# Softmax attention without row maxima, its exponentials shared by two engines, and linear attention laid under it by a list scheduler

## The chip, the cores and the metric

The program runs on one core of one Trainium2 chip. A core has five instruction streams that run side by side and meet only in semaphores: TensorE (PE, matrix products into PSUM), VectorE (DVE), ScalarE (ACT), GpSimd (POOL) and SyncE (SP, which here issues the DMAs). Each stream is executed in the order in which it was written. The metric is the device time of one execution in microseconds (us).

## The reference

Two attention layers over 2048 positions, 512 features and 32 heads of 16 features; their outputs stand side by side.

```
A:  q, k, v = split(x @ wqkv);  scores = q k^T * 0.25
    o = softmax(scores) v;      a = o @ wo
B:  q, k, v = split(x @ wqkv);  pq = q @ w_phi;  pk = k @ w_phi        (16x16 for each head)
    phi(t) = [softmax(t), softmax(-t)]                                 (32 features)
    kv = sum over positions of phi(pk) v;  z = sum over positions of phi(pk)
    o = phi(pq) kv / (phi(pq) z + 1e-6);   b = o @ wo
out = concat(a, b)                                                     (2048 x 1024, bfloat16)
```

A's softmax takes 32 x 2048 x 2048 exponentials, which are 1,048,576 columns on 128 partitions. All else is small beside it.

## The kernel before

**Units.** A is cut into 32 units: 8 groups of four heads times 4 blocks of 512 queries. A unit has 16 key tiles of 128 keys. The four heads of a group lie at partitions 0, 32, 64 and 96 of `QT` and `KT`, 16 rows of features each, so that four scores matmuls can use four row strips of PE's array.

**Two passes over the scores.** The first pass exists only for the row maximum. `emit_m1` (the matmul is L611) writes scores with queries on the partitions, two heads at a time into a pair of PSUM banks, and `emit_r1` (L623) has DVE reduce these 128x1024 scores to their maxima. `emit_mchain` (L634 on DVE, L644 to L646 on POOL) makes two bfloat16 numbers of the maximum, and `emit_qb` and `emit_qe` (L654, L661, L672) add them to `QT` as two extra features, so that the second pass yields scores with the maximum taken off. The second pass has keys on the partitions: `emit_m2` (L692), one 128x512 block for each head, `emit_exp` (L703) on ACT, and `emit_pv` (L718), four products in four column strips of the array, which add up in PSUM bank 7 over the 16 key tiles. `VP` holds ones beside the values, so that the sums of the softmax come out with the numerators.

```
t = P.op("act", lambda e: e.activation(                                        # emit_exp, L703
    pT[:, slot, :], PS[:, bank, :], ACT.Exp, scale=0.25), [m2_t[B], slot_reader.get(slot)])
...
r1[q1] = P.op("dve", lambda e: e.tensor_reduce(                                # emit_r1, L623
    part[:, u % 2, qt, 2 * half:2 * half + 2, kc], PS[:, 2 * half:2 * half + 2, :],
    AX.X, ALU.max), deps)
```

**End of a unit.** `emit_xev` (L755) copies the sums and numerators to `X`, four DMAs (L759) spread the sums to the partitions of the numerators in `Yd`, ACT makes reciprocals of them as Exp(-Ln) (L769, L777), and POOL multiplies (L779).

**Order.** A hand-written loop over slots sets it: a slot holds one pair of L611 matmuls and their reduction, two blocks of the second pass (43 slots behind), a `PV` group every second slot, and what is left over of PE's time is filled by `emit_fill` (L734, L745) with products of zeros. Projections (L231, L249) stand ahead and in the first slots.

**B.** Its inputs are loaded when A's projections are through. Its key side and 12 of 16 tiles of its query side are hooks in the slots behind A's last row maximum (`T0`), the others follow after A. For each tile of 128 positions `fm0` to `fm3` take maximum, minimum, two subtractions (L374 to L379), an exponential (L388), sums (L397), reciprocals (L400) and a product on POOL (L409).

Of the kernel before, what the change touches and what calls it, by code (L numbers as in the profile page):

```python
# [1 line left out]

# [3 lines left out]
ACT = mybir.ActivationFunctionType  # L6
ALU = mybir.AluOpType
AX = mybir.AxisListType
BF = mybir.dt.bfloat16
F32 = mybir.dt.float32  # L10


class _Tok:
# [35 lines left out]
class _Plan:  # L49
# [19 lines left out]
    def dma(self, queue_key, dma_key, fn, deps=()):  # L69
        q = self.streams[queue_key]  # L70
        d = self.streams[dma_key]
        need = q.merge(deps)
        d.seq += 1
        clock = dict(q.known)
        clock[dma_key] = d.seq
        q.items.append((fn, need, dma_key))
        return _Tok(dma_key, d.seq, clock)

    def emit(self, key, eng):
        for fn, need, inc_key in self.streams[key].items:  # L80
# [10 lines left out]
        return s.seq * s.step  # L91


def bass_concat_heads__softmax_full_mha__linear_kernel_hedgehog__prompt_kernel(
    nc, A_x, A_wqkv, A_wo, B_x, B_wqkv, B_w_phi, B_wo, out
):
    S = 2048
    H = 32
    assert tuple(A_x.shape) == (1, S, 512) and tuple(B_x.shape) == (1, S, 512)
# [18 lines left out]
    with contextlib.ExitStack() as es:  # L118
        block = es.enter_context(nc.Block())

        def sb(name, shape, dt):
            return es.enter_context(nc.sbuf_tensor(name, shape, dt))

        P = _Plan()
        for key in ("pe", "act", "dve", "pool"):
            P.add_stream(key, es.enter_context(nc.semaphore("s_" + key)))
        P.add_stream("sp", None)

        def dsem(name):
            P.add_stream(name, es.enter_context(nc.semaphore("d_" + name)), 16)  # L130
            return name

        PS = es.enter_context(nc.psum_tensor("PS", [128, 8, 512], F32))
        bank_reader = {}

        ones_t = sb("ones_t", [128, 128], BF)
# [718 lines left out]
        NR = 4  # L855
# [118 lines left out]

        final_waits = [k for k, s in P.streams.items() if s.step == 16 and s.seq > 0]

        @block.sync
        def _(e):
            P.emit("sp", e)
            for k in final_waits:  # L980
                e.wait_ge(P.streams[k].sem, P.total(k))

        @block.tensor
        def _(e):
            P.emit("pe", e)

        @block.scalar
        def _(e):
            e.preload_act_table_set("natural_log_exp_and_others")
            P.emit("act", e)  # L990

        @block.vector
        def _(e):
            P.emit("dve", e)

        @block.gpsimd
        def _(e):
            P.emit("pool", e)


# [26 lines left out]
```

## Time and profile before

| | |
|---|---|
| median of 3 runs | 1420.08 us (1416.58 to 1423.36) |
| profiled execution, span from the first to the last instruction | 1415.5 us |
| busy: PE, DVE, ACT, POOL | 1240.7, 1324.3, 1269.5, 156.8 us |
| row maxima, L623 on DVE | 1024 instructions, 1165.5 us busy |
| exponentials, L703 on ACT | 2048 instructions, 1087.7 us busy |
| products of zeros, L734 and L745 on PE | 5644 instructions, 473.7 us busy |

The profile gives one execution; its own time is its span, 1415.5 us, and 4.6 us less than the median of the runs. "Busy" is the union of an engine's instructions, so it is less than count times mean duration where instructions overlap at their edges. Line numbers (L623) are those of the kernel before; those of the changed kernel are named as such.

### The profile page before, as it was taken

The page shows a single profiled execution, that of the slowest core. Times are in us where ns is not written, and L with a number is a line of the kernel's source. Part 1 is how long each engine was busy: PE and PEld are TensorE (multiplying, and loading weights), DVE is VectorE, ACT ScalarE, POOL GpSimd, SP SyncE. Part 2 cuts the span into 40 slices and gives each one's busy share as a digit, 9 for nine tenths or more (in the row PEclk, how much of TensorE's full clock was granted, in tenths as well). Part 3 has the DMA queues.
Part 4 walks back from the last instruction along what each step waited for, and adds up shares of the span by engine and source line. Part 5 has one row for each costly group of instructions (what it writes and reads, how often), then busy time and mean ns, then how long its engine had stood idle before and what let it go on. Part 6 is the DMA issues. An engine that isn't in the chain of part 4 may idle for free.

```text
span 1415.5 us, 32468 instructions
## 1 busy us (share of the span) xinstructions
PE 1240.7 (88%) x13964; PEld 372.4 (26%) x13996; DVE 1324.3 (94%) x1333; ACT 1269.5 (90%) x2474; POOL 156.8 (11%) x257
## 2 busy tenths in 40 slices
PE   5998999998999988888888899998888998988766
PEld 2332322222222222222222222222222222233244
DVE  1499999999999999999999999999999999688978
ACT  3648999999999999999999999999999999877557
POOL 5000000000000000000000000000000000034432
PEclk9999999999999999999999999999999999999989
DMA  5006000000000000000000000000000000000001
GB/s 119 1 1 106 20 5 6 5 5 5 5 5 5 5 5 5 5 5 5 5 5 5 6 5 5 5 6 5 5 3 5 5 5 6 5 20 16 20 26 50
DMA packets 34480, 18.88 MB, mean 13 GB/s; under 512 B 25120, under 2 KB 32288, under 8 KB 34336
## 3 DMA queue, kind: packets, MB, share of 16 engines
q1 hardware_dynamic: 34336, 16.81, 5.3%
q8 instruction: 109, 1.79, 0.5%
q14 instruction: 35, 0.29, 0.1%
HBM read 3.16 MB, written 4.19 MB: 5 GB/s over the span
## 4 chain that ended last, share of the span: by engine, by line
DVE 81%; PE 11%; ACT 5%; issue 1%; SPq 1%; POOL 1%; DMA 0%; DVEq 0%; ACTq 0%; POOLq 0%
DVE part L623 76%; PE PS L249 4%; ACT pT L703 3%; PE PS L366 1%; PE PS L231 1%; PE PS L611 1%; PE PS L505 1%; DVE statK L397 1%; DVE tbK L379 1%; DVE statK L374 1%; DVE statK L375 1%; PE PS L420 1%; PE PS L692 1%; PE PS L960 1%; ACT ebK L388 0%
## 5 line engine op out<-in xcount | busy, mean ns | idle before, releaser
L623 DVE TENSOR_REDUCE part<-PS 128x2 f32<-128x1024 f32 x1024 | 1165.5, 1219 | 42.1 <-PE PS L611 38.5
L703 ACT ACTIVATE pT<-PS 128x512 bf16<-128x512 f32 x2048 | 1087.7, 605 | 30.2 <-PE PS L692 7.8
L692 PE MATMUL PS<-QT,KT 32*128 32x512 bf16 x2048 | 508.0, 386 | 20.3 <-ACT pT L703 12.5
L611 PE MATMUL PS<-KT,QT 32*128 32x512 bf16 x2048 | 397.3, 385 | 79.5 <-DVE part L623 67.9
L734 PE MATMUL PS<-zmv,ones_t 128*32 128x512 bf16 x5228 | 439.2, 383 | 0.0
L611 PEld LDWEIGHTS PS<-KT,QT 32*128 32x128 bf16 x2048 | 96.3, 91 | 532.9 <-DVE part L623 505.9
L718 PE MATMUL PS<-pT,VP 128*32 128x512 bf16 x2048 | 205.4, 391 | 17.0 <-ACT X L755 17.0
L692 PEld LDWEIGHTS PS<-QT,KT 32*128 32x128 bf16 x2048 | 140.4, 91 | 101.0 <-ACT pT L703 81.7
L779 POOL TENSOR_TENSOR QT<-X,Yd 128x256 bf16<-128x256 f32 x64 | 46.3, 723 | 740.7 <-ACT Yd L777 740.7
L734 PEld LDWEIGHTS PS<-zmv,ones_t 128*32 128x32 bf16 x5228 | 99.5, 95 | 97.0 <-issue 97.0
L718 PEld LDWEIGHTS PS<-pT,VP 128*32 128x32 bf16 x2048 | 52.6, 92 | 135.7 <-issue 109.8
L644 POOL TENSOR_SCALAR stage<-mrow 128x16 bf16<-128x16 f32 x32 | 10.0, 311 | 398.9 <-DVE mrow L634 398.9
L388 ACT ACTIVATE ebK<-tbK 128x1024 bf16<-128x1024 f32 x28 | 29.8, 1063 | 25.0 <-DVE tbK L379 24.6
L409 POOL TENSOR_TENSOR phikK<-ebK,statK 128x512 bf16<-128x512 bf16 x36 | 37.2, 1055 | 69.8 <-DVE statK L400 65.8
L249 PE MATMUL PS<-xAT,WKp 128*128 128x512 bf16 x125 | 30.7, 395 | 16.0 <-DVE WKp L200 15.9
L261 ACT ACTIVATE KT<-PS,bias_k 128x512 bf16<-128x512 f32 x32 | 22.0, 687 | 22.7 <-PE PS L249 22.7
L374 DVE TENSOR_REDUCE statK<-PS 128x32 f32<-128x512 f32 x28 | 18.6, 665 | 23.9 <-PE PS L366 23.7
L745 PE MATMUL PS<-zmv,ones_t 128*32 128x512 bf16 x416 | 34.5, 383 | 2.5
L257 ACT ACTIVATE QT<-PS 128x512 bf16<-128x512 f32 x32 | 19.1, 597 | 19.3 <-PE PS L249 19.3
L366 PE MATMUL PS<-WKp,xAT 128*128 128x512 bf16 x119 | 33.4, 402 | 2.6 <-issue 1.3
L249 PE MATMUL PS<-xAT,WQp 128*128 128x512 bf16 x125 | 33.7, 390 | 0.4 <-issue 0.3
L397 DVE TENSOR_REDUCE statK<-ebK 128x64 f32<-128x1024 bf16 x28 | 33.5, 1196 | 0.0
(89 smaller groups left out, 620.8 us busy)
## 6 DMA issues: line engine op xcount, KB each, us to landing
Yd<-X SPq DMA_DIRECT2D x128, 32.0 KB, 2.0
out_dram<-OA SPq DMA_DIRECT2D x16, 128.0 KB, 1.7
out_dram<-pT SPq DMA_DIRECT2D x16, 128.0 KB, 1.7
wA<-in_A_wqkv_dram SPq DMA_DIRECT2D x3, 512.0 KB, 4.3
WOp<-in_A_wo_dram SPq DMA_DIRECT2D x4, 128.0 KB, 6.2
wA<-in_B_wqkv_dram SPq DMA_DIRECT2D x1, 512.0 KB, 5.0
BD<-in_B_w_phi_dram SPq DMA_DIRECT2D x32, 0.5 KB, 1.5
woB<-in_B_wo_dram SPq DMA_DIRECT2D x1, 512.0 KB, 3.3
```

The lines of the kernel that those rows point to most:

```text
L249: tok = P.op("pe", lambda e, ct=ct: e.matmul(PS[:, b, :], wpad[:, ct, g, :], xAT[:, ct, c * 512:(c + 1) * 512], start=(ct == 0), stop=(ct ...
L366: tok = bank_task(bank, 4, lambda e, b, ct: e.matmul(PS[:, b, :], xBT[:, ct, st * 128:(st + 1) * 128], Wf[:, x, ct, :], start=(ct == 0), s ...
L397: t6 = P.op("dve", lambda e: e.tensor_reduce(ss, ebuf[:, ie, :].rearrange("p (g f) -> p g f", f=16), AX.X, ALU.add), [ctx["exp"]] + users. ...
L409: t8 = P.op("pool", lambda e, a=a: e.tensor_tensor(dv[:, a], ev4[:, a], rs3[:, a].unsqueeze(2).broadcast_to([128, 32, 16]), ALU.mult), [ct ...
L611: tok = P.op("pe", lambda e, r=r: e.matmul(PS[:, r, :], QT[32 * r:32 * r + 32, g, q0:q0 + 128], KT[32 * r:32 * r + 32, g, kc * 512:(kc + 1 ...
L623: r1[q1] = P.op("dve", lambda e: e.tensor_reduce(part[:, u % 2, qt, 2 * half:2 * half + 2, kc], PS[:, 2 * half:2 * half + 2, :], AX.X, ALU ...
L692: m2_t[B] = P.op("pe", lambda e: e.matmul(PS[:, bank, :], KT[32 * r:32 * r + 32, g, kt * 128:(kt + 1) * 128], QT[32 * r:32 * r + 32, g, c ...
L703: exp_t[B] = P.op("act", lambda e: e.activation(pT[:, slot, :], PS[:, bank, :], ACT.Exp, scale=0.25), [m2_t[B], slot_reader.get(slot)])
L718: tok = P.op("pe", lambda e, B=B, r=r: e.matmul(PVB[32 * r:32 * r + 32, :], VP[:, kt, 4 * g + r, :], pT[:, B % RING, :], start=(kt == 0), ...
L734: P.op("pe", lambda e, cq=cq: e.matmul(PVB[32 * cq:32 * cq + 32, :], ones_t[:, 0:32], zmv[:, :], start=False, stop=False, tile_position=(0 ...
L745: P.op("pe", lambda e, cq=cq: e.matmul(PS[32 * cq:32 * cq + 32, bank, :], ones_t[:, 0:32], zmv[:, :], start=True, stop=True, tile_position ...
L779: t = P.op("pool", lambda e: e.tensor_tensor(QT[:, g, lo:lo + 256], X[:, ub, sl], Yd[:, ub, sl], ALU.mult), [ex, xev_t[u], last_m2[u]])
```

## The change

The kernel of before stays in the program as `_general`, with every name prefixed, behind a branch. Ahead of it stands a new function, `_main_path`, which computes the whole result in another way; every engine then loads a flag and enters `_general` only if the flag is set.

- A without maxima: the first pass, the chain behind it, the two extra features and the products of zeros are gone. A scores block is made once, with keys on the partitions.
- On ACT an exponential now covers a pair of banks, 128x1024.
- Four of 16 key tiles of a unit (`DK`) are meant for DVE. `tensor_scalar` computes `ya * score + yb` from PSUM and writes it as uint16 (L613 of the changed kernel); those bits, read as bfloat16, are 2 to a power, with a straight line between powers of two. To even out the line's error six such values with shifted phases are added up: five more `tensor_scalar` add a whole number to the uint16 tile of 128x2048 and clamp it (L625), each shifted tile goes into a `PV` group of its own with values scaled to fit (`VJ`). A key tile on DVE so takes 2 conversions, 5 additions and 6 `PV` groups. Where ACT is through first, it takes a tile from DVE's list; in the built order that happens for one tile.
- A unit ends in a copy by DVE (L550), four DMAs that broadcast one row of sums to 16 partitions (L558) and four that collect the sums (L564), a `reciprocal` of 128x512 on DVE (L570) and a product on POOL (L572).
- B loses its maxima and minima, too. Its key side takes exponentials from PSUM on ACT (L781), sums and reciprocals on DVE (L787, L790), the product on POOL (L792); its query side takes transposed features (L874, L884), reciprocals and products from PSUM on DVE (L900, L903), nine small operations for each tile on POOL (L918 to L933).
- The order comes from a list scheduler, `_Sched`: each piece of work is a task with an engine, a duration from a table of constants in the code, its predecessors and the buffers that it needs; at each step the task that can start first is placed, by priority of its stream where several can. B's tasks have lower priorities than A's. The emitted streams are fixed; the chip waits by semaphores alone.
- At the end DVE counts sums that lie between 2^-40 and 2^40 (L983 to L993) and sets the flag.

```diff
+    def qk_task(u, kt, half, need, nbank):
+        g, c = units[u]
...
+            return e.matmul(PS[:, b, :], KT[32 * r:32 * r + 32, g, kt * 128:(kt + 1) * 128],
+                            QT[32 * r:32 * r + 32, c, g // 2, :], start=True, stop=True, tile_position=(32 * r, 0))
+        return _Task("pe", 0.28, pe_group(2, mm), [q_ready[(g // 2, c)], k_ready[(g, kt // 4)]], lat=0.2, need=need)
...
+    def act_kt(u, kt):
+        exps = []
+        for half in range(2):
+            qk = qk_task(u, kt, half, [("A", A_bank, 1, 1)], lambda t: 2 * t.res["A"].idx)
...
+                return e.activation(pT[:, t.res["p"].idx, :], PS[:, b:b + 2, :].rearrange("p a n -> p (a n)"),
+                                    ACT.Exp, scale=0.25)
+            exps.append(put(ac_ex, _Task("act", 0.957, one("act", ex_emit), [qk], lat=0.12,
+                                         need=[("p", pt_sl, 1, 1)], rel=[lambda qk=qk: [qk.res["A"]]])))
...
+    def dve_kt(u, kt):
+        npv[u] += _NPH - 1
+        firsts = []
+        for half in range(2):
+            qk = qk_task(u, kt, half, [("D", D_bank, 2, 1)], lambda t: 4)
...
+                return e.tensor_scalar(rg[:, firsts[0].res["i"].idx, 1024 * half:1024 * half + 1024],
+                                       PS[:, 4:6, :].rearrange("p a n -> p (a n)"), ya, yb, ALU.mult, ALU.add)
+            firsts.append(put(dv_a, _Task("dve", 1.19, one("dve", cv), [qk], lat=0.1,
+                                          need=[("i", ri_sl, 1, _NPH)] if half == 0 else [],
...
+        for j in range(1, _NPH):
+            ad = put(dv_ad, _Task("dve", 0.61, one("dve", lambda e, t, j=j: e.tensor_scalar(
+                rg[:, t.res["j"].idx, :], rg[:, firsts[0].res["i"].idx, :], float(sh[j]), 32767.0, ALU.add, ALU.min)), firsts, lat=0.1,
+                need=[("j", rj_sl, 1, 1)], rel=[lambda: [firsts[0].res["i"]]]))
+            put(pe_pd, pv_task(u, kt, [ad, vj_ready[(kt, j)]],
+                               lambda h, j=j: VJ[:, j - 1, k, 17 * h:17 * h + 32],
...
+            rc = put(dv_n, _Task("dve", 0.62, one("dve", lambda e, t: e.reciprocal(
+                Yd[:, yi(), :], Yd[:, yi(), :])), [sh_], lat=0.1))
+            mul[u] = put(po_n, _Task("pool", 1.4, one("pool", lambda e, t: e.tensor_tensor(
+                OT[:, g, :], X[:, xi, :], Yd[:, yi(), :], ALU.mult)), [rc] + op_done.get(c - 1, []), lat=0.1,
...
+        def guard(e, fn):
+            with e.If(e.value_load(flag[0:1, 0:1])):
+                for k in ends:
+                    e.wait_ge(P0.streams[k].sem, P0.total(k))
+                fn(e)
```

In the built order the changed path has 254 conversions, 635 additions, 32 long reciprocals and 140 copies of 512 columns from PSUM on DVE; 770 exponentials of 1024 columns on ACT; 1024 pairs of scores matmuls and 1147 groups of `PV` on PE.

What the order does on DVE: before, the end of A's row maxima and the first tile of B (`part` maxima by block, `mrow` maxima by unit, `statK` and `tbK` B's maxima and differences):

```order
L623 TENSOR_REDUCE part<-PS 128x2 [waits s_pe] x30
L634 TENSOR_REDUCE mrow<-part 128x16 [waits s_dve]
L374 TENSOR_REDUCE statK<-PS 128x32 [waits s_pe]
L375 TENSOR_REDUCE statK<-PS 128x32
L377 TENSOR_TENSOR tbK<-PS,statK 128x512 [waits s_dve]
L379 TENSOR_TENSOR tbK<-statK,PS 128x512 [waits s_dve]
```

Now, around the end of a unit in the middle of A (`X` and `Yd` as before, `rg` the uint16 tiles):

```order
L550 COPY X<-PS 128x512 [waits s_pool,d_col1,s_pe]
L613 TENSOR_SCALAR rg<-PS 128x1024
L625 TENSOR_SCALAR rg<-rg 128x2048
L613 TENSOR_SCALAR rg<-PS 128x1024 [waits s_pe]
L570 RECIPROCAL Yd<-Yd 128x512 [waits d_sh0]
L625 TENSOR_SCALAR rg<-rg 128x2048 [waits s_pe]
L625 TENSOR_SCALAR rg<-rg 128x2048
```

The reductions are gone, B's tiles no longer stand behind them, and the reciprocal stands in line with conversions and additions, three instructions behind the copy whose row it needs by DMA (`d_sh0`).

What it does on PE: before, a stretch of the middle of A (`zmv` and `ones_t` are the products of zeros):

```order
L611 MATMUL PS<-KT,QT 128x512 [waits s_dve]
L611 MATMUL PS<-KT,QT 128x512
L692 MATMUL PS<-QT,KT 128x512 [waits s_act] x2
L718 MATMUL PS<-pT,VP 32x512 x4
L734 MATMUL PS<-zmv,ones_t 32x512 x4
```

Now, a stretch of the middle of A (L515 scores, L523 `PV`, from ACT's `pT` or DVE's `rg`):

```order
L515 MATMUL PS<-QT,KT 128x512 [waits s_act]
L515 MATMUL PS<-QT,KT 128x512
L523 MATMUL PS<-pT,VP 32x512 x4
L523 MATMUL PS<-rg,VP 32x512 x4
L523 MATMUL PS<-rg,VJ 32x512 [waits s_dve]
L523 MATMUL PS<-rg,VJ 32x512 x3
L515 MATMUL PS<-QT,KT 128x512 [waits s_act]
L515 MATMUL PS<-QT,KT 128x512
L515 MATMUL PS<-QT,KT 128x512 [waits s_dve]
L515 MATMUL PS<-QT,KT 128x512
```

Scores for ACT and scores for DVE, and the products of both, now stand in one line, so that a matmul that waits for DVE holds up the scores for ACT that stand behind it.

More of the change, by code (lines that the diff above doesn't have):

```diff
@@ L10 @@
 F32 = mybir.dt.float32
+U16 = mybir.dt.uint16
+I32 = mybir.dt.int32
 class _Tok:
@@ L91, in total, with __init__, take, drop @@
         return s.seq * s.step
-def bass_concat_heads__softmax_full_mha__linear_kernel_hedgehog__prompt_kernel(
-    nc, A_x, A_wqkv, A_wo, B_x, B_wqkv, B_w_phi, B_wo, out
-):
+class _Slot:
+    __slots__ = ("idx", "free", "toks", "left", "next")
+    def __init__(self, idx):
+        self.idx = idx
+        self.free = 0.0
+        self.toks = []
+        self.left = 0
+        self.next = []
+    def take(self, n):
+        toks = self.toks
+        self.toks = []
+        self.next = []
+        self.left = n
+        return toks
+    def drop(self, tok, end):
+        self.next.append((tok, end))
+        self.left -= 1
+        if self.left == 0:
+            self.free = max(e for _, e in self.next)
+            self.toks = [k for k, _ in self.next]
@@ new lines, with __init__ @@
+class _Task:
+    __slots__ = ("eng", "dur", "lat", "deps", "emit", "need", "tok", "end", "res", "then", "rel", "done", "pre")
+    def __init__(self, eng, dur, emit, deps=(), lat=0.0, need=(), rel=(), then=None, pre=()):
+        self.eng = eng
+        self.dur = dur
+        self.lat = lat
+        self.emit = emit
+        self.deps = [d for d in deps if d is not None]
+        self.need = list(need)
+        self.rel = list(rel)
+        self.then = then
+        self.pre = list(pre)
+        self.res = {}
+        self.tok = None
+        self.end = None
+        self.done = False
```

775 lines of the change are left out of this document (763 added, 12 removed).

## The prediction

> **What bounds the kernel now.** I read the page first (busy shares and the chain that ended last), then the chain in order of time, then the groups of instructions by form, then single stretches.
>
> ```profile
> span 1415.5 us, 32468 instructions
> PE 1240.7 (88%) x13964; PEld 372.4 (26%) x13996; DVE 1324.3 (94%) x1333; ACT 1269.5 (90%) x2474; POOL 156.8 (11%) x257
> DVE  1499999999999999999999999999999999688978
> ACT  3648999999999999999999999999999999877557
> DVE 81%; PE 11%; ACT 5%; issue 1%; SPq 1%; POOL 1%; DMA 0%; DVEq 0%; ACTq 0%; POOLq 0%
> ```
>
> Three engines look full, but the chain runs over DVE for 81% of the span. The stretch that repeats shows why:
>
> ```profile
> 609.39 36.20 DVE part L623 x32
> 300.00:336.30 36.30, 32.65 (x397) 8.80 (x396) 36.30 (x34) 35.38 (x72) 2.29 (x5) 1.00 0.02 5
> ```
>
> The first line is the chain in order of time, the second a window of one unit (PE, PEld, DVE, ACT, POOL busy, granted clock, DMA share, GB/s). A unit takes 36.3 us, all of them DVE's: 32 row-max reductions at 36.20/32 = 1.131 us. ACT has 35.38 of 36.30 and would bind next. Outside this stretch lie loads and projections, the first two digits of DVE's row, and the bulk of B, its last six, where neither engine stays at 9.
>
> **Prices.** Groups by form, columns: count, then busy us and mean ns of one.
>
> ```profile
> L623 DVE TENSOR_REDUCE part<-PS 128x2 f32<-128x1024 f32 x1024 | 1165.5, 1219 | 42.1 <-PE PS L611 38.5 <-PE PS L692 0.9
> L397 DVE TENSOR_REDUCE VP<-KT 128x64 f32<-128x1024 bf16 x4 | 4.8, 1210 | 0.0
> L939 DVE TENSOR_TENSOR VP<-PS,VP 128x256 bf16<-128x256 f32 x32 | 12.1, 420 | 0.6
> L400 DVE RECIPROCAL statK<-statK 128x64 f32<-128x64 f32 x28 | 15.5, 553 | 1.0
> L935 DVE RECIPROCAL VP<-VP 128x32 f32<-128x32 f32 x16 | 5.6, 353 | 0.5
> L200 DVE COPY WQp<-wA 128x2048 bf16<-128x2048 bf16 x1 | 0.7, 694 | 3.7 <-DMA wA<-in_A_wqkv_dram 3.7
> L200 DVE COPY WKp<-wA 128x2048 bf16<-128x2048 bf16 x1 | 0.9, 883 | 5.3 <-DMA wA<-in_A_wqkv_dram 5.3
> L703 ACT ACTIVATE pT<-PS 128x512 bf16<-128x512 f32 x2048 | 1087.7, 605 | 30.2 <-PE PS L692 7.8
> L672 ACT ACTIVATE QT<-PS 128x256 bf16<-128x256 f32 x64 | 25.1, 392 | 0.0
> L354 ACT ACTIVATE VP<-PS 128x1024 bf16<-128x1024 bf16 x16 | 16.4, 1032 | 1.5 <-PE PS L909 1.5
> L779 POOL TENSOR_TENSOR QT<-X,Yd 128x256 bf16<-128x256 f32 x64 | 46.3, 723 | 740.7 <-ACT Yd L777 740.7
> L409 POOL TENSOR_TENSOR QT<-KT,VP 128x512 bf16<-128x512 bf16 x8 | 8.3, 1057 | 32.2 <-DVE VP L933 32.2
> L644 POOL TENSOR_SCALAR stage<-mrow 128x16 bf16<-128x16 f32 x32 | 10.0, 311 | 398.9 <-DVE mrow L634 398.9
> ```
>
> And single instructions of DVE, PE and SP in order of time (start, us):
>
> ```profile
> 1394.86 0.68 DVE L375 TENSOR_REDUCE VP<-PS 128x32 f32<-128x512 f32 x1
> 1395.46 0.68 DVE L377 TENSOR_TENSOR KT<-PS,VP 128x512 f32<-128x512 f32 x1
> 599.72 0.39 PE L692 MATMUL PS<-QT,KT 32*128 32x512 bf16 x1
> 600.03 0.62 PE L734 MATMUL PS<-zmv,ones_t 128*32 128x512 bf16 x8
> 601.01 0.40 PE L718 MATMUL PS<-pT,VP 128*32 128x512 bf16 x4
> 601.23 0.39 PE L734 MATMUL PS<-zmv,ones_t 128*32 128x512 bf16 x4
> 623.97 2.41 SPq L759 DMA_DIRECT2D Yd<-X  x4
> ```
>
> Queued DVE instructions follow each other about 0.08 us sooner than they last (1.131 against 1.219; starts 0.60 apart against 0.68), ACT's by 0.605 - 1087.7/2048 = 0.074. I count steps start to start.
>
> **Removed.** Row maxima, 1024 x 1.131 = 1158 us of DVE, and with them the binding chain; half of PE's scores; on ACT the Ln and Exp of each unit, and B's passes of maxima and differences.
>
> **ACT now.** 256 columns more cost 605 - 392 = 213 ns, so 1024 columns last 605 + 426 = 1031 ns (L354's 1032 agrees) and step at 0.957. 770 of them are 737 us in place of 1088; four evacuations of 1024 columns and 96 other instructions of 512 at 0.53 are 55 more. ACT: 792 us.
>
> **DVE now.**
> (a) Conversions: 254, one float column from PSUM per step as the reduction reads it, at 1.13: 287 us.
> (b) Additions: 635 over 2048 two-byte columns in SBUF. Nothing in this trace adds uint16. From below the copy of 2048 bfloat16 columns, 694 ns, step 0.61, 390 us; from above one column at a time as L397 reads bfloat16, twice 1.21 less the fixed part, 2.26 us, 1435 us. I take the copy: one source, one constant pair, SBUF to SBUF, the same 2048 columns of two bytes.
> (c) Long reciprocals: from 32 to 64 columns L935 and L400 grow by 200 ns, 6.25 ns a column and 153 ns fixed. For 512 columns that is 3.35 us, step 3.27, and 32 of them 105 us. The scheduler's table holds 0.62 for it. The lower end is that figure of one column per step, as in L375, 0.60, or 19 us; I take 3.27, since both rows are of this very operation.
> (d) 140 copies of 512 columns from PSUM at 0.60: 84 us.
> (e) B and the rest: key tiles 16 x (1.12 sums + 0.47 reciprocal + 0.35 two small ones) = 31; query tiles 16 x (0.64 for three reciprocals of 24, 24 and 16 columns, 1.36 for products of 408, 408 and 272 columns drawn from L939's 256, 0.42 for two small ones) = 39; memsets, x copies and checks 11. Together 81 us.
> Sum of (a) to (e): 947 us. DVE stays the longest engine, and most of its gap to ACT is the reciprocal, which the scheduler did not see: by its figure (c) would be 20.
>
> **PE now.** From a scores matmul to the first column-strip group behind it 600.03 - 599.72 = 0.31 us pass, between groups of one kind 0.22. 1024 pairs, 1147 groups and 640 full matmuls at 0.22 are 618; the built order changes kind 1778 times, at 0.09 each 160; small matmuls about 40. PE: 820 us, under DVE's.
>
> **What DVE loses beside its own work.**
> DMAs (issue to landing, us; then duration of an issue, min/median/max in ns), and POOL's memsets in the same form:
>
> ```profile
> Yd<-X SPq DMA_DIRECT2D x128, 32.0 KB, 2.0
> ...
> L318 SPq DMA_TRANSPOSE xAT<-in_B_x_dram x4: 1942/2104/3598, 105.4 to 113.2; - x4
> ...
> L324 SPq DMA_TRANSPOSE WQp<-in_B_wqkv_dram x8: 1193/1261/1972, 115.9 to 125.7; - x8
> ...
> L208 POOL MEMSET VP<- x16: 519/519/1061, 10.5 to 18.0; 128x512 bf16 x16
> ```
>
> The reciprocal waits for a DMA whose four issues take 2.41 us (row 623.97), the last landing 2.0 behind its issue. So the row of sums is there about 3.9 us after the copy to `X`, but the three instructions ahead of the reciprocal cover 1.13 + 0.61 + 1.13 = 2.9. Some 1.0 us x 32 = 32 us of waiting; between nothing (smaller DMAs) and 60. Queued behind it are conversions and additions, for which PE's products and, behind those in PE's line, the scores for ACT wait. B's twelve transposed loads stand on SP ahead of one unit's DMAs: 4 x 2.1 + 8 x 1.26 = 19 us, once; the unit lasts longer (its DVE work alone is 8 x 1.13 + 20 x 0.61 + 3.27 + 0.6 = 25), so nothing, and 19 at the most.
>
> POOL and DVE disturb each other. The second copy of L200 took 883 ns, not 694, while POOL was in L208's row of memsets, and one of these took 1061 ns, not 519. So a wide DVE copy waits for POOL's instruction to end, and POOL's for the copy. The additions are of this kind. POOL's new work is 32 products of 512 columns at 2 x 0.72 = 46 us, 16 of 1024 at 2.1 = 34, B's nine small ones in 16 tiles about 4.4 each = 70, and 12 for `VJ`: 162 us. DVE loses between 0 and 162; an addition is next on DVE about half of the time, and part of POOL's instruction is over or beside a conversion by then, so I take 50. [...]
>
> Windows of the B stretch of before (columns as above), and DVE's first instruction on loaded data:
>
> ```profile
> 1300.00:1340.00 40.00, 29.64 (x326) 12.15 (x333) 37.73 (x57) 24.44 (x39) 18.66 (x19) 1.00 0.06 18
> 1340.00:1380.00 40.00, 25.79 (x272) 15.74 (x274) 31.38 (x66) 21.12 (x32) 15.59 (x16) 0.83 0.08 27
> ...
> 8.88 0.69 DVE L200 COPY WQp<-wA 128x2048 bf16<-128x2048 bf16 x1 [3.69 <-DMA wA<-in_A_wqkv_dram]
> ```
>
> Other waits: three engines that meet in one PE line. In the B stretch, where this is so, DVE was busy 37.73 of 40 and 31.38 of 40 us, in the fully fed unit 36.30 of 36.30. Between 0 and 21%; A has deeper buffers than that stretch, so I take 5% of 947, 48 us.
> Ends: first data reached DVE at 8.88 us, and x now has to be transposed by PE ahead of the first projection: 10 us of waiting. Behind the last addition come copy, DMA, reciprocal, product, four output tiles that share one PSUM bank, checks and the branch: some 25 us, of which DVE's own is counted; 18. The check and the branch appear in no row; bounded by 0 and, as a matmul and six small steps, 6 us. The fallback's code costs nothing if it isn't entered, since no engine passes through it.
>
> **Sum.** 947 + 32 + 50 + 48 + 28 = 1105 us of span against 1415.5; the runs lie 4.6 us above the profiled span, so 1110 us. B's work, which stood behind A's row maxima, is now inside DVE's sum.
>
> **Rivals.**
> 1. *The waits nearly vanish, or the long reciprocal is short.* With DVE at 947 + 28 and none of the three losses the span is 975, with a reciprocal at 0.60 too 890. For it: the order has other DVE work at almost every point. Against: two rows on the reciprocal, and DVE's copy that did wait for POOL. Below 1000: 0.12.
> 2. *The engines run in lockstep, and PE's clock falls.* The order is fixed for a reciprocal of 0.62. Each then comes 2.65 us late, PE stops at a product that needs DVE, ACT at scores behind that; if PE and ACT cannot catch up, their own unevenness adds to DVE's. The products of zeros that kept PE busy are gone, too: the clock was 1.00 with them and 0.83 at 25.79 of 40 us busy in the row of 1340. At 0.83 PE's 820 become 988, next to DVE's 947, and two engines that alternate so give about 1230; up to 1350. [...] Against: PE still has work in 820 of 1105 us, and needs no more than that. 0.15.
> 3. *The additions don't run as the copy did.* This ends on the other side. At one column per step they take 2.26 us, (b) is 1435 and the time about 2150. It decides from 635 x d = 1420 - 1110, that is when an addition steps at 0.61 + 0.49 = 1.10 us, about two columns per step. For it: no integer operand and no two-operation instruction of this width is in the trace. Against: the copy of the same width. Slower than 1420: 0.05.
> 4. *The check fails and the old path runs behind the new:* 1110 + 1415, about 2530. Scores are small here (x and w of scale 0.05), sums lie near 2048, far inside 2^-40 to 2^40. 0.01; some other trouble beyond 1427, 0.01.
>
> **How the numbers follow.** Forecast, DVE binds with moderate losses, 1000 to 1200: 0.66. With rivals 1 and 2 on its sides, 985 to 1230 holds about 0.8: the lower end is all losses near nothing, the upper is POOL's whole 162 us, or PE's clock at 0.83. No change that a measurement can tell means within 0.5%, 1413 to 1427: 0.01. Faster 0.92, slower 0.07.
>
> **What the profile of the changed kernel would show.** Right: DVE above 85% busy and first in the chain, ACT near 790 us and PE's own work well under the span; additions near 0.69 us at the median, with a tail up to 2 us where POOL is at work; long reciprocals at 3.35 us, each ahead of an idle stretch of PE and ACT; DVE waiting about 1 us for the DMA ahead of them. Wrong: additions at 1.1 us and more; reciprocals at 0.6; a granted clock under 0.9 with DVE idle behind PE; the old path's lines in the trace.

## The result, and the profile after

The changed kernel takes 1303.33 us (median of 4 runs, 1293.74 to 1312.18) against 1419.33 us (1416.58 to 1423.36) of the kernel before: ratio 0.9182, 95% interval 0.9124 to 0.924. It is faster, as forecast, but 193 us slower than the 1110 us that I forecast, and outside the range of 985 to 1230. `_general` was not entered.

The head of the page of the changed kernel: span, busy time of each engine, three rows of the 40 slices, the granted clock, and the share of the engines in the chain that ended last.

```profile
span 1291.9 us, 19102 instructions
PE 1047.3 (81%) x8077; PEld 259.5 (20%) x8077; DVE 1019.4 (79%) x1271; ACT 804.5 (62%) x871; POOL 217.9 (17%) x241
PE   7979477978889679878888888887898888887974
DVE  3797589888774896988887888888787888888872
ACT  5736346666565466677767676667666577666730
PEclk9997678777666786677778887889777788788775
PE 44%; DVE 36%; DMA 8%; SPq 6%; issue 3%; POOL 1%; ACT 1%; POOLq 0%; DVEq 0%
```

Before, DVE was at 9 in 32 slices on end. Now no engine is: PE and DVE stand at 7 to 9 in most slices, ACT at 5 to 7. The chain passes from one to the other, and DMAs with their issues on SP (SPq) hold 14% of it. The clock, which was 1.00 wherever I had looked at A before, is 0.773 over the span of this execution, the fastest of the four.

Groups by form of the changed kernel, columns as before (count, busy us, mean ns of one, idle time ahead of them and who ended it), and the DMA issues' row with the time to landing:

```profile
L594 ACT ACTIVATE pT<-PS 128x1024 bf16<-128x1024 f32 x770 | 751.8, 1029 | 388.4 <-PE PS L515 238.0
L625 DVE TENSOR_SCALAR rg<-rg 128x2048 uint16<-128x2048 uint16 x635 | 452.0, 744 | 49.2 <-PE PS L523 40.2
L613 DVE TENSOR_SCALAR rg<-PS 128x1024 uint16<-128x1024 f32 x254 | 308.2, 1213 | 37.7 <-PE PS L515 36.5
L523 PE MATMUL PS<-rg,VJ 128*32 128x512 bf16 x2540 | 288.8, 467 | 164.7 <-DVE rg L625 163.1
L570 DVE RECIPROCAL Yd<-Yd 128x512 f32<-128x512 f32 x32 | 107.3, 3353 | 86.5 <-DMA Yd<-X 86.5
...
Yd<-X SPq DMA_DIRECT2D x128, 32.0 KB, 3.2
```

The reciprocal takes 3353 ns, and DVE waits for its DMA for 86.5 us. PE waits 163 us for additions, ACT 238 us for scores. The chain in order of time (start, us, what) shows one unit from its end to the next:

```profile
580.98 0.61 DVE X L550
581.61 0.52 SPq L558
...
583.44 3.32 DMA Yd<-X
586.78 3.35 DVE Yd L570
590.13 2.22 DVE rg L625 x2
592.40 0.62 PE PS L523 x4
...
602.34 0.69 DVE rg L625
...
611.85 0.61 DVE X L550
```

The end of a unit, from the copy to the end of the reciprocal, is a chain of 9.1 us (580.98 to 590.13). Beside it DVE still has conversions and additions, and stands still for the last 1.12 us ahead of the reciprocal. Then comes PE, for ten microseconds (592.40 to 602.34), then DVE, until the next copy, 30.87 us after the first. Windows of the same unit and of a longer stretch (PE, PEld, DVE, ACT, POOL busy, granted clock, DMA share, GB/s):

```profile
582.00:592.00 10.00, 7.12 (x54) 1.56 (x52) 8.36 (x7) 5.82 (x6) 1.58 (x1) 0.67 0.25 14
592.00:602.00 10.00, 9.60 (x70) 1.80 (x70) 7.63 (x10) 6.04 (x6) 0.00 (x0) 0.51 0.01 2
602.00:612.00 10.00, 8.85 (x90) 2.40 (x82) 9.66 (x14) 9.87 (x11) 0.00 (x0) 1.00 0.00 0
...
482.00:508.00 26.00, 26.00 (x212) 5.84 (x210) 18.49 (x26) 17.41 (x17) 0.00 (x0) 0.50 0.00 1
```

Behind the reciprocal PE is busy for 9.60 of 10 us, but at half clock; DVE and ACT wait for it. At full clock, in the third row, DVE and ACT are both nearly full. The last row is 26 us out of the longest such stretch of A, with no gap on PE, all at 0.50.

### The profile page after: what moved, and what is told of

Its sections match the earlier page's. It is cut to its first block, busy times and chain, and to the rows that moved or that the text cites. A ratio compares the mean times of both kernels' runs of the same rounds, so it can differ in the third digit from the quotient of the medians.

```text
span 1291.9 us, 19102 instructions
## 1 busy us (share of the span) xinstructions
PE 1047.3 (81%) x8077; PEld 259.5 (20%) x8077; DVE 1019.4 (79%) x1271; ACT 804.5 (62%) x871; POOL 217.9 (17%) x241
## 4 chain that ended last, share of the span: by engine, by line
PE 44%; DVE 36%; DMA 8%; SPq 6%; issue 3%; POOL 1%; ACT 1%; POOLq 0%; DVEq 0%
PE PS L523 17%; PE PS L515 14%; DVE rg L625 12%; DMA Yd<-X 8%; DVE Yd L570 8%; DVE rg L613 8%; SPq L558 4%; PE PS L670 3%; PE PS L442 3%; PE PS L874 2%; DVE X L550 1%; DVE rmin L798 1%; PE PS L439 1%; PE PS L803 1%; PE PS L948 1%
## 5 line engine op out<-in xcount | busy, mean ns | idle before, releaser
L594 ACT ACTIVATE pT<-PS 128x1024 bf16<-128x1024 f32 x770 | 751.8, 1029 | 388.4 <-PE PS L515 238.0
L625 DVE TENSOR_SCALAR rg<-rg 128x2048 uint16<-128x2048 uint16 x635 | 452.0, 744 | 49.2 <-PE PS L523 40.2
L515 PE MATMUL PS<-QT,KT 32*128 32x512 bf16 x2048 | 410.1, 459 | 28.6 <-ACT pT L594 13.4
L523 PE MATMUL PS<-rg,VJ 128*32 128x512 bf16 x2540 | 288.8, 467 | 164.7 <-DVE rg L625 163.1
L613 DVE TENSOR_SCALAR rg<-PS 128x1024 uint16<-128x1024 f32 x254 | 308.2, 1213 | 37.7 <-PE PS L515 36.5
L570 DVE RECIPROCAL Yd<-Yd 128x512 f32<-128x512 f32 x32 | 107.3, 3353 | 86.5 <-DMA Yd<-X 86.5
L523 PE MATMUL PS<-pT,VP 128*32 128x512 bf16 x1540 | 171.6, 468 | 2.4 <-DVE X L550 2.4
L515 PEld LDWEIGHTS PS<-QT,KT 32*128 32x128 bf16 x2048 | 86.4, 94 | 367.1 <-issue 157.7
L572 POOL TENSOR_TENSOR OT<-X,Yd 128x512 bf16<-128x512 f32 x32 | 49.4, 1544 | 542.9 <-DVE Yd L570 542.9
L523 PEld LDWEIGHTS PS<-rg,VJ 128*32 128x32 bf16 x2540 | 65.1, 100 | 309.6 <-DVE rg L625 243.4
L918 POOL TENSOR_TENSOR w<-w 128x204 f32<-128x204 f32 (+1 forms) x48 | 38.7, 806 | 294.5 <-DVE w L903 294.5
L523 PE MATMUL PS<-rg,VP 128*32 128x512 bf16 x508 | 64.0, 495 | 0.0
L670 PE MATMUL PS<-WOp,OT 128*128 128x512 bf16 x128 | 51.6, 533 | 13.4 <-POOL OT L572 10.9
L523 PEld LDWEIGHTS PS<-pT,VP 128*32 128x32 bf16 x1540 | 38.3, 98 | 119.4 <-issue 106.0
L792 POOL TENSOR_TENSOR w<-zb,stat 128x1024 bf16<-128x1024 bf16 x16 | 35.1, 2194 | 122.9 <-DVE stat L790 122.9
L874 PE MATMUL PS<-xT,Wfq 128*128 128x512 bf16 x128 | 45.6, 443 | 0.8 <-ACT zb L884 0.4
L933 POOL TENSOR_TENSOR w<-w,den 128x192 bf16<-128x192 f32 (+1 forms) x48 | 37.0, 796 | 10.4 <-DVE den L928 7.0
L781 ACT ACTIVATE zb<-PS 128x512 bf16<-128x512 f32 x32 | 17.4, 596 | 21.2 <-PE PS L772 21.2
```

What stands on the lines that cost most here:

```text
L515: return e.matmul(PS[:, b, :], KT[32 * r:32 * r + 32, g, kt * 128:(kt + 1) * 128], QT[32 * r:32 * r + 32, c, g // 2, :], start=True, stop= ...
L523: return e.matmul(PS[32 * r:32 * r + 32, 6, :], lhs(8 * (g // 2) + 2 * r + g % 2), rhs(r), start=t.res["first"], stop=t.res["last"], tile_ ...
L570: rc = put(dv_n, _Task("dve", 0.62, one("dve", lambda e, t: e.reciprocal(Yd[:, yi(), :], Yd[:, yi(), :])), [sh_], lat=0.1))
L572: mul[u] = put(po_n, _Task("pool", 1.4, one("pool", lambda e, t: e.tensor_tensor(OT[:, g, :], X[:, xi, :], Yd[:, yi(), :], ALU.mult)), [rc ...
L594: return e.activation(pT[:, t.res["p"].idx, :], PS[:, b:b + 2, :].rearrange("p a n -> p (a n)"), ACT.Exp, scale=0.25)
L613: return e.tensor_scalar(rg[:, firsts[0].res["i"].idx, 1024 * half:1024 * half + 1024], PS[:, 4:6, :].rearrange("p a n -> p (a n)"), ya, y ...
```

## Experiments

The theory to test had two parts. *Order:* the scheduler laid the order out with 0.62 us for a reciprocal that lasts 3.35 and with 2.2 us (0.3 on SP) for a transfer whose four issues and landing take some 5.2 (in the rows above, from the end of the copy at 581.59 to the reciprocal at 586.78), so that each unit's end stops DVE, behind it PE, behind that ACT. *Clock:* the stops halve PE's clock, and that costs the time. All times are medians; ratios are to the kernel before.

**e1, the scheduler told the reciprocal's length**

```diff
-            rc = put(dv_n, _Task("dve", 0.62, one("dve", lambda e, t: e.reciprocal(
+            rc = put(dv_n, _Task("dve", 3.3, one("dve", lambda e, t: e.reciprocal(
```

> One number changes: the scheduler is told 3.3 us for the long reciprocal in place of 0.62; every instruction stays, its place in the lines may move. Theory O (the order was laid out for a wrong duration, so PE stops behind each reciprocal): the stops go, DVE's idle time falls from 272 us by about 32 x 2.7 = 87, time about 1200. Theory C (PE's clock is halved because nothing fills its gaps, and PE at half clock binds, whatever the order): gaps around the end of a unit remain (copy to X, DMA), the clock stays under 0.85, time 1260 to 1310.

1273.02 us (1270.03 to 1283.58), ratio 0.8974 [0.8931, 0.9016], clock 0.759; the DMA waits of DVE are still 72.6 us. That is in the range of theory C, and far from the 1200 of theory O. The 30 us are the table's error on the reciprocal alone; the stop stays.

**e2, told the transfer's time too** (beside e1's edit)

```diff
-            sh_ = put(sp_q, _Task("sp", 0.3, dma(..., bc, 4), [xv], lat=2.2,
+            sh_ = put(sp_q, _Task("sp", 0.3, dma(..., bc, 4), [xv], lat=5.0,
```

> As e1, and the scheduler is told 5.0 us instead of 2.2 for the DMAs that spread the sums (measured: 5.2 from the end of the copy to the start of the reciprocal). Theory O: DVE's 86 us of waiting for these DMAs go as well, time about 1130. Theory C: clock under 0.85, time 1240 to 1310.

1218.17 us (1216.2 to 1220.56), 0.8575 [0.8549, 0.8601], between the two expectations. DVE's waits for the transfer in e1 and then in e2 (us in total, times, longest):

```profile
DVE Yd L570 <- DMA Yd<-X: 72.6, 32, 15.7
DVE Yd L570 <- DMA Yd<-X: 21.3, 3, 15.8
```

They fall by 51 us and the time by 55: about one for one. But the clock is 0.770, and PE has 53% of the chain. The reciprocal still keeps DVE for 107 us.

**e3, the reciprocal on ACT** (with 5.0 for the transfer; as Exp(-Ln), as in the kernel before)

```diff
-            rc = put(dv_n, _Task("dve", 0.62, ... e.reciprocal(Yd[:, yi(), :], Yd[:, yi(), :])), [sh_], lat=0.1))
+            ln = put(ac_rc, _Task("act", 0.6, ... e.activation(Yd[:, yi(), :], Yd[:, yi(), :], ACT.Ln)), [sh_], lat=0.12))
+            rc = put(ac_rc, _Task("act", 0.6, ... e.activation(Yd[:, yi(), :], Yd[:, yi(), :], ACT.Exp, scale=-1.0)), [ln], lat=0.12))
```

> As e2, but the reciprocal is taken by ScalarE as Exp(-Ln), two instructions of 512 columns; DVE loses 107 us of work, ScalarE gains about 35. Theory O: no long instruction is left on DVE, time 1030 to 1090. Theory C: the clock stays under 0.85 and PE's line of about 820 us at full clock takes 1000 or more, time 1150 or more.

1048.6 us (1047.28 to 1057.68), 0.7394 [0.736, 0.7429], as theory O had it. This is the best version, 26% under the kernel before and 20% under the changed one. The page of e3, and a window of it:

```profile
PE 925.6 (88%) x8077; PEld 252.3 (24%) x8077; DVE 897.1 (86%) x1239; ACT 828.5 (79%) x935; POOL 214.1 (20%) x241
PEclk9999768766868977958899999999999999999866
PE 45%; DVE 42%; POOL 3%; ACT 3%; issue 3%; SPq 2%; DMA 1%; POOLq 0%; DVEq 0%
```

```profile
560.00:640.00 80.00, 76.37 (x700) 20.65 (x696) 74.41 (x99) 75.19 (x86) 7.81 (x9) 1.00 0.12 13
```

In this stretch all three engines are over 92% busy at full clock; in the first half of A the clock is still lower. PE's busy time is 122 us less than in the changed kernel for the same matmuls (8077 in both). That is the clock: by the trace's clock records PE was busy for 478 us at half clock in the changed kernel and for 194 in e3, and with these counted half the work is 808 and 829 us. The two activations last 0.63 us each: ACT does in 40 us what cost DVE 107.

**e4, the stops filled.** The order of the changed kernel, with four matmuls of zeros ahead of every `PV` group from DVE that is not a unit's first, to see whether the clock alone makes the loss.

```diff
+            if fill and u in started and l_wo.done:
+                for i in range(4 * fill):
+                    P.op("pe", lambda e, r=i % 4: e.matmul(PS[32 * r:32 * r + 32, 6, :], zst[:, 0:32], WOp[:, 0, :],
+                        start=False, stop=False, tile_position=(0, 32 * r), ...), ...)
```

> The order of the changed kernel, with one group of four matmuls by zeros (into the open PV bank, changing nothing) ahead of each PV group that takes DVE's values, 635 groups, 140 us of PE at full clock. Theory C: PE stays active, granted clock 0.9 or more, time under 1240. Theory O: the stops behind the reciprocal are what they were, PE has more to do, time 1290 to 1400.

1308.22 us (1306.16 to 1315.28), 0.9217 [0.9184, 0.925]; a miss for the clock as the whole cause. It holds 762 such groups, not the number that the expectation has, 168 us of PE at 0.22. The clock went up from 0.773 to 0.896, the time not down. A single PE row shows that the stop itself did not go:

```profile
583.99 0.62 PE L525 MATMUL PS<-rg,VJ 128*32 128x512 bf16 x4 [3.80 <-DVE rg L633]
```

(L525 here is L523 of the changed kernel, L633 its L625.) One group of 0.22 us ahead of a wait of 3.8 cannot fill it; the groups raised the clock elsewhere, but PE's busy time went up by 47 us (1047.3 to 1094.4).

**e5, a short reciprocal in the old order.** 80 of 512 columns; the other 432 are left out.

```diff
-                Yd[:, yi(), :], Yd[:, yi(), :])), [sh_], lat=0.1))
+                Yd[:, yi(), 0:80], Yd[:, yi(), 0:80])), [sh_], lat=0.1))
```

> The changed kernel with its order untouched; the long reciprocal covers 80 of 512 columns (the other columns are left as they are), so that it lasts about 0.65 us, near the 0.62 that the order was laid out for. Theory S (the reciprocal costs its own length and no more): 32 x 2.7 = 86 us less, about 1217, granted clock as before, under 0.80. Theory K (each reciprocal stops PE behind it, the clock halves, and PE at half clock holds up DVE and ScalarE for some 10 us more): 1150 or less, clock 0.85 or more.

1184.84 us (1175.72 to 1195.15), 0.8325 [0.827, 0.838], clock 0.812: between the two expectations. DVE's busy time falls by 86.6 us (1019.4 to 932.8), the time by 118: the reciprocal costs its length and a third more. DVE's wait for the DMA is unchanged, 88.9 us.

**e6, no split.** All 1024 exponentials on ACT, in the scheduler's order.

```diff
-    DK = (3, 7, 11, 15)
+    DK = ()
```

> The changed kernel with an empty list of key tiles for VectorE: all 1024 exponential instructions run on ScalarE, 980 us at 0.957, and 55 of other work; the long reciprocals stay on VectorE, which then has some 270 us of work and never holds up the line. If the split itself pays in the changed kernel: slower than 1303. If the split's gain (ScalarE 243 us less) is lost again to the coupling of three engines in PE's line: 1080 to 1150, with ScalarE over 90% busy.

1378.28 us (1372.47 to 1381.98), 0.9716 [0.9684, 0.9748]. Busy times and clock of e6:

```profile
PE 1093.0 (80%) x5537; PEld 234.8 (17%) x5537; DVE 296.9 (22%) x382; ACT 1053.1 (77%) x1125; POOL 142.1 (10%) x221
PEclk9965555555556555555569755686555655555555
```

ACT has 1053 us of work, yet the span is 1370.7. DVE is busy for 297 us and has 7% of the chain, the transfers and their issues another 7%; the largest share is PE's, 52%. PE is at half clock in most of the slices and is busy for 1093 us with 5537 matmuls, where the changed kernel has 8077 in 1047. The split of the exponentials brings 75 us in the changed kernel (1378 to 1303), and leaves ACT 250 us of work less.

**e7, without B.** The tasks of B are left out.

```diff
-        if c == 1:
-            start_bq()
...
-    pj_last[-1].then = lambda _: start_b()
```

> The changed kernel without B: nothing of B is loaded or computed, its half of the output is not written. If B's work lies hidden under A: 1270 to 1303. If what it takes of VectorE (about 90 us) and of PE (about 130 us at full clock, more at the granted one) lies on the path: 1100 to 1200.

1177.47 us (1170.37 to 1195.02), 0.8282 [0.8233, 0.833], clock 0.677. B costs 126 us; it is not hidden under A. Without it the clock is lower still (0.773 to 0.677) and PE has 56% of the chain, though it has 1056 matmuls fewer.

**e8, e3 with all durations told.** Measured values in the table for additions (0.66), conversions (1.15), B's reciprocals and POOL's operations.

```diff
-                    ... _Task("pool", 0.9, one("pool", lambda e, t, j=j: ...
+                    ... _Task("pool", 1.6, one("pool", lambda e, t, j=j: ...
...
-            ad = put(dv_ad, _Task("dve", 0.61, ...
+            ad = put(dv_ad, _Task("dve", 0.66, ...
```

> e3 (reciprocal on ScalarE, DMA duration told) with the scheduler also told the measured durations of the additions, conversions, B's short reciprocals and products and GpSimd's operations. If wrong durations still cost something in e3: 1000 to 1035. If e3's rest is due to the engines' own work and PE's clock: 1040 to 1060.

1087.88 us (1067.06 to 1099.62), 0.7662 [0.7608, 0.7716]: slower than e3 in every run, by 18 to 51 us against e3's median, with the same own work (DVE 897.9), and outside both expectations. A truer table does not by itself make a better order; errors of some 0.04 to 0.7 us are not what cost the time. It shows, too, that a newly laid order alone can move the time by tens of us. The differences between versions with different tables (e1, e2, e3, e12, e13) can hold such a part, which was not taken apart; e5, in the order of the changed kernel, cannot.

**e9, e6 filled.** Groups of zeros as in e4 ahead of the scores for ACT, 958 of them.

> e6 (all exponentials on ScalarE) in its order, with one group of four matmuls by zeros ahead of each pair of scores matmuls while the PV bank is open: 958 groups, 211 us of PE at full clock. PE's own work in e6 is small and its clock was 0.58. Theory C: with the gaps filled the clock is 0.9 or more, a scores pair takes its 0.39 us, ScalarE works nearly without a break (980 + 55 + ends), time 1100 to 1170. Theory O (the clock is only a sign of waiting, the fixed order sets the time): 1370 or more.

1411.12 us (1397.01 to 1477.21, 5 runs), 0.9887 [0.9842, 0.9933], clock 0.746 against 0.581. Another miss of the fill; the time is above 1370, as theory O had it. Windows of e9, and then PE's rows in order of time:

```profile
504.00:708.00 204.00, 201.29 (x1229) 35.24 (x1228) 19.88 (x10) 155.69 (x159) 6.34 (x5) 0.50 0.06 4
708.00:712.00 4.00, 4.00 (x19) 0.81 (x18) 0.35 (x1) 2.20 (x3) 0.00 (x0) 0.57 0.39 28
```

```profile
708.50 0.61 PE L528 MATMUL PS<-QT,KT 32*128 32x512 bf16 x2
709.04 1.89 PE L690 MATMUL PS<-WOp,OT 128*128 128x512 bf16 x4
710.86 0.61 PE L528 MATMUL PS<-QT,KT 32*128 32x512 bf16 x2
711.40 0.40 PE L540 MATMUL PS<-pT,VP 128*32 128x512 bf16 x4
```

PE was busy for 201 of 204 us and the clock stayed at 0.50 all the while; the longest such stretch without a gap is about 40 us. It came back at 711 us, behind four matmuls over the whole array (L690, 128*128); the others are pairs in row strips (L528) and fours in column strips (L540 and the zeros). So here a full PE line, as the profile counts it, did not by itself bring the clock back.

**e10, e3 filled in the first 18 units** (426 groups), where e3's clock is low.

> e3 with one such group ahead of each PV group on VectorE's values in units 0 to 17, where e3's clock is low: 426 groups, 94 us of PE at full clock. Theory C: clock 0.95, time 1000 to 1035. Theory O: 1049 to 1090.

1084.9 us (1083.26 to 1086.94), 0.7639 [0.7617, 0.7662], clock 0.932 against 0.888: slower by 36 us, as theory O had it.

**e11, e5 filled** (762 groups).

> e5 (reciprocal over 80 of 512 columns, order of the changed kernel) with such a group ahead of each PV group on VectorE's values, 762 groups, 168 us of PE at full clock. Both suspects are taken away in the changed kernel's own order. Theory C: clock 0.95, time 1110 to 1150, against 1185 without. Theory O: 1185 to 1230.

1180.17 us (1176.61 to 1184.55), 0.8314 [0.8281, 0.8346]. Clock and chain of e11:

```profile
PEclk9999779999798898999999999999999999999997
PE 57%; DVE 21%; DMA 9%; SPq 6%; issue 4%; ACT 3%; POOL 1%; POOLq 0%; DVEq 0%
```

The clock is 0.95 against 0.812, and the time that of e5 (1184.84), just under the range of theory O. Of the chain, 15% are the transfers and their issues, 177 us or 32 x 5.5. The fills fell as a cure four times: each time PE's busy time went up, by 17 us here and by 159 in e9, so that the groups took more of PE's line than the clock gave back. They do not say what a full clock for nothing would bring. What they do show is that the transfer stays on the chain at a clock of 0.95, too.

Still open then was how the wait for the transfer, the reciprocal and the clock divide the loss.

**e12, both stops out of DVE's line** (e5's short reciprocal and e2's 5.0 for the transfer).

> The order is laid out with a DMA latency of 5.0 us instead of 2.2 in its table, and the reciprocal on VectorE covers 80 of 512 columns, so that the rest of it is left out. Theory 'two stops that add': the unit's end holds DVE up once by the transfer (86.5 us of waits in the changed kernel) and once by the 3.35 us of the reciprocal, and each is lost several times over through PE's line and its clock. With both gone the time is that of the version with the reciprocal on ScalarE, 1030 to 1090 us, and DVE's waits on DMA are under 20 us. Rival 'the reciprocal alone': once the reciprocal is short the transfer's wait is covered by slack, and the time stays at that of the short reciprocal in the old order, 1160 to 1200.

1055.22 us (1053.54 to 1056.53), 0.7428 [0.7407, 0.7449], clock 0.885. Page and waits of e12:

```profile
PE 932.7 (89%) x8077; PEld 255.6 (24%) x8077; DVE 909.3 (86%) x1271; ACT 793.0 (75%) x871; POOL 213.3 (20%) x241
PE 47%; DVE 40%; ACT 3%; POOL 3%; SPq 2%; issue 2%; DMA 1%; POOLq 0%; DVEq 0%
L570 DVE RECIPROCAL Yd<-Yd 128x80 f32<-128x80 f32 x32 | 20.6, 644 | 18.7 <-DMA Yd<-X 18.7
```

The time and the wait are where the theory had them; the rival, 1160 to 1200, falls. The two stops more than add: the short reciprocal takes 118 us off (e5), the 5.0 alone 55 beside the long reciprocal (e1 to e2), both together 248. With the exponentials still shared as in the changed kernel and one number and one width altered, 1055 us are left of 1303.

**e13, e3 with the old 2.2 for the transfer**

> Reciprocal as two activations on ScalarE, with the DMA latency of 2.2 us left in the table. Theory 'two stops that add': ScalarE's line now has the wait for the transfer that VectorE's had, some 2 to 3 us in each unit; against 1049 us with 5.0 in the table that gives 1080 to 1150. Rival 'only VectorE's line matters', because ScalarE has less work of its own: 1040 to 1060.

1106.88 us (1103.53 to 1110.54), 0.7785 [0.7757, 0.7812], clock 0.844. As the theory had it: the wait has moved to ACT's line, and against e3's 18.2 us there 56 us more of it cost 58.

```profile
L570 ACT ACTIVATE Yd<-Yd 128x512 f32<-128x512 f32 x32 | 20.2, 630 | 74.6 <-DMA Yd<-X 74.6
```

**e14, e3 with three key tiles on DVE**

```diff
-    DK = (3, 7, 11, 15)
+    DK = (4, 9, 14)
```

> The best version so far (reciprocal on ScalarE, 5.0 us in the table, 1049 us) with three of 16 key tiles of a unit on VectorE instead of four. By own work: PE has 32 x 5 groups less (about -38 us from 926), DVE 32 x (2 x 1.13 + 5 x 0.70) = 184 us less (from 897 to 713), ACT 32 x 2 x 0.957 = 61 more (from 829 to 890). Theory 'PE is the bound of that version': PE's 38 us come off, 1000 to 1035. Rival 'ScalarE's line becomes the bound', since it now has the most work after PE and waits for PE in every unit: 1050 to 1090.

1092.4 us (1084.86 to 1103.14), 0.7681 [0.7625, 0.7737]. Neither expectation is met (the second ends 2 us lower, but has ACT as the bound): the clock fell to 0.815, so PE, with 620 matmuls fewer, was busy for 960 us, 34 more than in e3, and has 53% of the chain against ACT's 13%. DVE waits for it ahead of a unit's copy:

```profile
DVE X L550 <- PE PS L523: 98.2, 19, 16.8
```

Fewer groups did not relieve PE. Why the clock is lower there was not tried.

The cells of the study side by side:

| reciprocal | transfer 2.2 in the table | transfer 5.0 | gain of 5.0 |
|---|---|---|---|
| DVE, 3.35 us, table 3.3 | 1273 (e1) | 1218 (e2) | 55 |
| DVE, 0.64 us, table 0.62 | 1185 (e5) | 1055 (e12) | 130 |
| ACT, 2 x 0.63 us | 1107 (e13) | 1049 (e3) | 58 |

## Why the prediction was right or wrong

**Right: what is removed, and the own work.** DVE's own work with POOL's share was to be 997 us and is 1019.4. The long reciprocal was worked out at 3.35 us from two narrower rows and is 3353 ns, in all 32 cases. ACT was to have 792 us and has 804.5. Additions run about as the copy did, 683 ns at the median against 694; rival 3 is out, and so is rival 4. POOL does hold up DVE. Of these rows of DVE in order of time the first stands where POOL is idle, the second where POOL's product (L572) runs:

```profile
609.96 1.88 DVE L625 TENSOR_SCALAR rg<-rg 128x2048 uint16<-128x2048 uint16 x3
620.90 2.90 DVE L625 TENSOR_SCALAR rg<-rg 128x2048 uint16<-128x2048 uint16 x3
```

and of these two groups of the same operation and size the first runs behind the sums of B's key side, when POOL takes up products of 2.2 us (L792), the second on the query side:

```profile
L798 DVE TENSOR_TENSOR rmin<-rmin,stat 128x64 f32<-128x64 f32 x16 | 24.2, 1515 | 0.0
L910 DVE TENSOR_TENSOR rmin<-rmin,stat 128x64 f32<-128x64 f32 x16 | 4.6, 288 | 0.0
```

Three additions take 1.0 us more beside the product, and L798 five times what L910 takes. Over the whole trace an addition with no POOL instruction beside it lasted 621 to 696 ns, one with a POOL instruction beside it up to 1755, and 73 of the 75 above 760 ns ended 0.55 us behind the end of a POOL instruction; conversions lasted 1211 ns at the median beside POOL and 1215 without. I had 50 us for this; the own work with it came out 22 us too small.

**Mis-sized: the wait for the transfer, 32 us, measured 86.5.** Two errors. I took 2.0 us to landing from the kernel before, where it was the median of the four DMAs that spread the sums from 16 rows to 16 partitions; now that one row goes to 16 partitions it is 3.2, and 31 of the waits come to 2.2 us on average, not 1.0. And SP's twelve transposed loads, "so nothing, and 19 at the most", cost nearly the most, once:

```profile
113.67 10.36 SPq L709 DMA_TRANSPOSE w<-in_B_wqkv_dram  x8
125.80 12.01 SPq L722 DMA_TRANSPOSE xT<-in_B_x_dram  x4
143.18 3.35 DVE L570 RECIPROCAL Yd<-Yd 128x512 f32<-128x512 f32 x1 [16.97 <-DMA Yd<-X]
```

The issues of that unit's DMAs stood behind 22.4 us of other issues. That a unit lasts longer than that is no cover: the reciprocal's place in DVE's order is fixed, and it waits there.

**Mis-sized: the ends, 28 us, measured 54.** DVE is busy for 57.27 of the first 88 us and 8.79 of the last 31.9:

```profile
0.00:88.00 88.00, 76.29 (x483) 22.85 (x484) 57.27 (x77) 50.63 (x59) 41.83 (x47) 1.00 0.21 50
...
1260.00:1291.90 31.90, 13.19 (x31) 3.54 (x31) 8.79 (x15) 0.00 (x0) 1.26 (x1) 0.55 0.11 26
```

**Failed: "other waits", 5% of 947 or 48 us, and the sentence that PE "needs no more" than 820 of 1105 us.** DVE's idle time is 272.5 us; without the ends and the transfer (84 outside the ends) 135 are left, of which some 77 are the waits of additions and conversions for PE in the rows of L625 and L613. The four differences, 22 in the own work, 52, 26 and 87, are the 187 us by which the span exceeds 1105. The step that failed is the one that priced PE at full clock and so kept it off the path. The work itself was priced well: counted half where the clock was half, it is the 808 us given with e3, against 820. At the clock that it had, PE was busy for 1047 us, and it has the largest share of the chain. This is rival 2, which stood at about 1230, up to 1350, and had 0.15: a reciprocal that comes late by 2.65 us, PE stopped, the clock down (0.83 assumed, 0.773 measured), two engines that alternate. The time lies inside its price, and its chance was too small. Its cause is only a part of what the runs show: it names the reciprocal and the table, not the transfer, and telling the table the reciprocal's length took off 30 us (e1). The fixed order, the table's 0.62 and the clock's row of the B stretch were all in front of me. What I set against it, that PE has slack on average, is an average over stages: within a unit the slack lies in the wrong ten microseconds.

By the experiments the two stops are the root: with both out of DVE's line the same division of work takes 1055 (e12), or 1049 with a reciprocal that is still computed (e3). That the time is then under the forecast of 1110 agrees with the own work in the sum: without the long reciprocals, e3's DVE has 897 us. The stops cost more than their length: from the changed kernel to e12 DVE lost 110 us of work (87 of reciprocal, 24 of additions, which last 707 ns there and not 744) and 68 us of waits for the transfer, 178 together, and the time fell by 248. The rest, 70 us, goes with PE's busy time, 115 us less for the same matmuls. That the half clock carries these 70 us is consistent with all runs but not shown by itself, since every fill that raised the clock (e4, e9, e10, e11) took PE's time in exchange.

That B's work is inside DVE's sum was right in kind: taking B out takes 119 us off DVE's busy time (1019.4 to 900.1) and 126 off the time (e7). In size it was short, since I had some 70 us of B in the own work and part of the 50 for POOL. Of what the profile was to show, the additions' and the reciprocal's durations, ACT's work and the idle stretches behind the reciprocal came out; DVE above 85% busy and first in the chain did not, and of the signs listed as wrong, "a granted clock under 0.9 with DVE idle behind PE" did.

## What to carry to other kernels

Where three engines meet in one in-order line, price each repeated stop by what stands behind it, not by its length alone, and read the cover of a transfer from the place of its reader in the order, not from the length of the stage. A table that sets an order needs the long items right (here one reciprocal and one transfer: 85 us from the changed kernel to e2); sharpening the short ones brought nothing (e8). Taking the long operation off the line brought more than telling the table of it: 170 us from e2 to e3. Before filling an idle engine to hold its clock, take away what makes it idle, and look for an engine on which the late operation is short: two activations of 0.63 us did what one reciprocal of 3.35 us did.

## What the runs showed of the hardware

- The clock came in steps. Added up from windows of one microsecond, as in these four of e4, where 2 x (0.28 + 0.50 + 0.50 + 0.43) is 3.42 us, each stage at half clock in the changed kernel, but the one that the program's end cuts, lasts a multiple of about 3.4 us: 3.4, 6.8, 10.2, 13.7, 17.1, up to 37.5.

```profile
348.00:349.00 1.00, 0.32 (x4) 0.14 (x8) 1.00 (x2) 0.00 (x0) 0.08 (x1) 0.72 0.00 0
349.00:350.00 1.00, 1.00 (x12) 0.16 (x4) 1.00 (x2) 0.00 (x0) 0.00 (x0) 0.50 0.00 0
350.00:351.00 1.00, 1.00 (x10) 0.21 (x6) 1.00 (x3) 0.00 (x0) 0.00 (x0) 0.50 0.00 0
351.00:352.00 1.00, 1.00 (x6) 0.13 (x2) 0.56 (x1) 0.71 (x1) 0.00 (x0) 0.57 0.00 0
```

  A busy PE did not end such a stage at once: 26 us in the changed kernel and 204 us in e9 stayed at 0.50 with PE busy for 26.00 and 201.29 us of them in the profile (whose ends of matmuls are modelled). Nor did the clock come back only behind matmuls over the whole array, as at 709 us in e9: cut into steps of 3.4 us, the stages at half clock of the changed kernel hold 43 steps that had no gap on PE and in which no such matmul started, and behind 11 of them the clock was full. What brings it back is not shown.
- At half clock a change of kind between groups took 0.54 us start to start (710.86 to 711.40 in e9), against 0.31 at full clock in the trace of before (599.72 to 600.03).
